# Output products of 14 of 18 token tiles by seven products of a Strassen level, with the output weights decoded earlier and kept in DRAM, and two first-layer units of 384 columns

## The chip, the cores and the metric

The kernel runs as one program on one core of a Trainium2 chip. The metric is the time of one execution on the device in microseconds (us): before the change three runs took 1123.82, 1124.44 and 1125.28 us, median 1124.44. Engines are named as in the profile: PE (matrix multiplication; PEld are its loads of the stationary operand), DVE (vector), ACT (scalar, activations), POOL (GpSimd) and SP (which issues the DMAs). SBUF is the on-chip memory, PSUM the eight banks into which PE accumulates, each 128 x 512 fp32.

## The reference

Attention with a bias made by a small network, then a layer `h - tanh(h)`, then a gated layer. Everything is fp32 at the interface; the weights come as float64.

```python
attn = softmax(q @ k.T / 8 + bias)            # 4 batches, 8 heads, 576 tokens, 64 wide
x = (attn @ v) as 2304 tokens x 512
h = x @ w_in;  x = (h - np.tanh(h)) @ w_out   # 512 -> 2048 -> 512
g = x @ w_gate                                # 512 -> 1536
silu = g * (1.0 / (1.0 + np.exp(-g)))
val = x @ w_val                               # 512 -> 1536
return silu * val @ w_out2                    # 1536 -> 512
```

## The kernel before, in words

Every product that needs fp32 accuracy is made of three PE instructions (`matmul3`, L719): both operands are split into a high part, rounded to PE's fp32r format, and the low rest; high x high, high x low and low x high are summed in PSUM. The split costs one cast on ACT (`scalar.copy`) and one subtraction on DVE or POOL (`subtract`, L64).

The first layer (class `Moe`, L746) takes the tokens in five units, `UNITS` (L734): four of 512 columns and one of 256. An item is one unit with one of the 16 chunks of 128 hidden columns. An item has 12 matmuls into `h` (`hidden`), a chain on ACT and DVE (`tanh_first`, `tanh_second`), the split of its result into `gh` and `gl` (`split`, L857 on ACT, L64 on POOL), and 12 matmuls into four banks `y` (`project`). Four chunks make a group; after each group the banks are added to `acc` in SBUF (L884). `ORDER` and `LAST_ORDER` (L735) are the order of the units in a group: the 256 unit third, in the last group first. `combine_x` (L984) queues the casts and subtractions that turn finished columns of `acc` into operands of the second layer; `flush(n)` emits n of them after each item (L1486).

The second layer (class `Second`, L945) works in 36 steps n: a set of 256 columns of the gate or value weights (set n // 3) against 768 tokens (n % 3). Steps 0 to 5 are plain blocks; from step 6 on (`step`, L1281) each 2 x 2 block product is done with seven products instead of eight, Strassen's scheme in Winograd's form. PE's order in a step is P1(n), P2(n-1), P4(n-1), P6(n), P3(n-1), P5(n), P7(n), with sums of partial results on ACT and DVE (`copy_one`, `copy_two`, `add`, `point_one`). `copy_two` (L1190) reads the bank into which P7(n) then accumulates. The gated result `s` goes to DRAM. The weights of a set are decoded from float64 bits to fp32 by two ACT, three DVE and one POOL instructions per 128 x 512 piece (`decode_first` L1052, `decode_second` L1063), then split and combined (`combine_w`). `plan_decode` (L1118) writes down for each set in which step and which part of the step (0, 1, 2) these stand.

The last product, `s` times `w_out2`, begins in `finish` (L1388). It has 18 token tiles of 128 and 12 chunks of 128 rows of `w_out2`; tiles are taken in waves of 8, 8 and 2, a stage is one chunk with one wave. `stage_load` brings `s` back from DRAM, `stage_split` casts and subtracts, and `out_tiles` multiplies: three matmuls of 512 columns for each tile and chunk. `w_out2` is decoded here too, one piece per step or stage from step 32 on (`FIRST_O`), and stays split in SBUF slots (`OUT_SLOTS`, `split_out`). `evict` copies a finished tile to SBUF and stores it. Each engine runs its instructions in the order in which this code emits them; the SP queue issues all DMAs in order.

Of the kernel before, what the change touches and what calls it, by code (L numbers as in the profile page):

```python
# [9 lines left out]
F32 = mybir.dt.float32  # L10
# [723 lines left out]
UNITS = [(0, 512), (512, 512), (1024, 512), (1536, 512), (2048, 256)]  # L734
ORDER, LAST_ORDER = (0, 1, 4, 2, 3), (4, 0, 1, 2, 3)  # L735
# [10 lines left out]
class Moe:  # L746
# [169 lines left out]
U2 = 384  # L916
# [5 lines left out]
OUT_SLOTS = (  # L922
    (16, 17), (18, 19), (27, 28), (29, 9), (20, 21), (22, 23), (24, 25), (26, 8), (0, 1), (2, 3), (4, 5), (6, 7),
)
QUAD_BANKS = (("h2", "h0", "h1"), ("h3", "y0", "y1"))
# [3 lines left out]
WAVES = ((0, 8), (8, 8), (16, 2))  # L929
LAST_C = 4  # L930
FIRST_O = 31
# [13 lines left out]
class Second:  # L945


    def __init__(self, tc, moe, weights, w_gate, w_val, w_out2, out):
# [7 lines left out]
        self.todo = [p for s in self.sets for p in s] + self.outs  # L956
# [7 lines left out]
    def pools(self, ctx):  # L964
        dram = ctx.enter_context(self.tc.tile_pool(name="c_dram", bufs=1, space=DRAM))
        self.s = [dram.tile([128, NT], F32, name=f"s_{c}") for c in range(FF2 // 128)]

# [16 lines left out]
    def combine_x(self, p):  # L984
# [28 lines left out]
        mixed = V if p == 2 else G  # L1013
# [97 lines left out]
    def split_out(self, c):  # L1111

        q = self.outs[c]
        q["pair"] = to = [self.columns(2 * at, 512) for at in OUT_SLOTS[c]]
        self.nc.scalar.copy(to[0], q["w"])
        subtract(self.nc, to[1], q["w"], to[0].bitcast(F32))

    def plan_decode(self):  # L1118
# [3 lines left out]
        for s in range(len(self.sets)):  # L1122
# [7 lines left out]
        for c, q in enumerate(self.outs):  # L1130
            n = FIRST_O + c
            add(n + 2, 0, self.split_out, c)
            add(n + 1, 1, self.decode_second, q)
            add(n + 1, 0, self.decode_first, q)
# [146 lines left out]
    def step(self, n):  # L1281
# [22 lines left out]
        if n == NQ - 1:  # L1304
            self.stage_split(0, 0, 768)
# [14 lines left out]
    def place(self, f, low):  # L1320

        return self.moe.x[low][:, f % 2, 0:1024]

    def raw(self, f):
        z = f % 3
        return self.moe.x[z // 2][:, 2 + z % 2, 0:1024].bitcast(F32)

    def stage_load(self, f, a=0, b=1024):

        if f >= len(self.stages):  # L1330
            return
        w, cs = self.stages[f]
        t0 = 128 * WAVES[w][0]
        if len(cs) == 1:
            self.nc.sync.dma_start(out=self.raw(f)[:, a:b], in_=self.s[cs[0]][:, t0 + a:t0 + b])
        else:
            n = 1024 // len(cs)
            for k, c in enumerate(cs):
                self.nc.sync.dma_start(out=self.raw(f)[:, n * k:n * k + n], in_=self.s[c][:, t0:t0 + n])

    def stage_split(self, f, a=0, b=1024):

        if f < len(self.stages):
            raw, hi, lo = self.raw(f)[:, a:b], self.place(f, 0)[:, a:b], self.place(f, 1)[:, a:b]
            self.nc.scalar.copy(hi, raw)
            subtract(self.nc, lo, raw, hi.bitcast(F32), self.nc.vector)

    def rows(self, at):

        z, k = divmod(at % 9, 3)  # L1350
# [4 lines left out]
    def out_tiles(self, f, ts=None):  # L1355

        nc = self.nc
        w, cs = self.stages[f]
        first, nt = WAVES[w]
        n = 1024 // len(cs)  # L1360
        s = self.place(f, 0), self.place(f, 1)
        for t in range(nt) if ts is None else ts:
            at = first + t
            if cs[0] == 0:
                self.o[at] = self.bank(OUT_BANKS[at % 8], f"o_{at}")
            for k, c in enumerate(cs):
                x = n * k + 128 * t
                matmul3(
                    nc, self.o[at], [a[:, x:x + 128] for a in s], self.outs[c]["pair"], c == 0, c == len(self.outs) - 1,
                )  # L1370
            if cs[-1] == len(self.outs) - 1:
                self.evict(at)
# [170 lines left out]
```

## Time and profile before

| | before |
|---|---|
| median of three runs | 1124.44 us |
| the profiled execution | 1124.47 us |
| its span, first to last instruction | 1122.7 us |
| PE busy | 1105.2 us, 98% of the span |
| DVE, ACT, POOL busy | 77%, 68%, 42% |
| mean granted clock | 0.999 |

The span is 1.8 us shorter than the execution. Busy time of PE is counted from the start of a matmul to its modelled end; matmuls overlap, so the pace of PE is read from start to start. First-layer items run from about 293 to 693 us, the steps of the second layer from 693 to 976 us, the output product from 968 us to the end.

### The profile page before, as it was taken

Reading aid. Unit: us, or ns where it says so; the run is one execution under the profiler, and the core shown is the slowest. Engines: PE = TensorE matmul, PEld = TensorE weight load, DVE = VectorE, ACT = ScalarE, POOL = GpSimd, SP = SyncE. Lnnn points to the kernel's source line nnn. Section 1 sums busy time; section 2 is a strip of 40 time slices with the busy share of each in tenths; the row PEclk is TensorE's granted clock in tenths of the full one; section 3 lists DMA queues with packets and bytes.
Section 4 is the critical chain, followed back from the end, with each engine's and each line's share of the span. In section 5 each row is a group of like instructions: output and inputs, shape, how many; then the busy total and the mean of one; then the engine's idle time right before and its main releaser. Section 6 shows DMA issues by size and latency. Waiting matters only on the chain.

```text
span 1122.7 us, 21424 instructions
## 1 busy us (share of the span) xinstructions
PE 1105.2 (98%) x7772; PEld 924.8 (82%) x7772; DVE 863.5 (77%) x1691; ACT 765.2 (68%) x1530; POOL 476.6 (42%) x499
## 2 busy tenths in 40 slices
PE   7999999999999999999999999999999999999998
PEld 3477777777688888888888888999999999988887
DVE  8978999999798889889988888987667665774222
ACT  7989999999698877777777776545455445453112
POOL 2367777777455355354434343124223222351000
PEclk9999999999999999999999999999999999999999
DMA  5863535351111111101101010131422422763433
GB/s 196 292 176 94 158 81 168 83 172 54 49 58 57 39 57 54 41 20 57 57 19 39 19 38 1 36 126 57 141 94 67 141 85 87 251 197 107 155 94 113
DMA packets 93034, 107.47 MB, mean 96 GB/s; under 512 B 45312, under 2 KB 72064, under 8 KB 92928
## 3 DMA queue, kind: packets, MB, share of 16 engines
q1 hardware_dynamic: 92928, 106.10, 30.1%
q8 instruction: 61, 1.00, 0.4%
q14 instruction: 45, 0.37, 0.1%
HBM read 75.41 MB, written 30.67 MB: 94 GB/s over the span
## 4 chain that ended last, share of the span: by engine, by line
PE 85%; DVE 8%; ACT 3%; issue 1%; POOL 1%; DMA 1%; DVEq 0%; ACTq 0%; POOLq 0%
PE b L722 19%; PE h L722 17%; PE y L722 16%; PE o L722 13%; PE x L438 7%; PE s L317 6%; PE pTa L383 2%; DVE acc L64 1%; PE pTb L383 1%; ACT p L343 1%; DVE r L146 1%; PE pE L400 1%; DVE p L332 1%; DVE xl L64 1%; DMA bias<-bev 1%
## 5 line engine op out<-in xcount | busy, mean ns | idle before, releaser
L722 PE MATMUL y<-gh,w 128*128 128x512 f32 (+1 forms) x748 | 197.0, 368 | 0.0
L722 PE MATMUL h<-xh,w 128*128 128x512 f32 (+1 forms) x640 | 191.0, 369 | 0.0
L722 PEld LDWEIGHTS y<-gh,w 128*128 128x128 f32 x748 | 133.9, 188 | 24.3 <-POOL gh L64 0.5
L722 PEld LDWEIGHTS h<-xh,w 128*128 128x128 f32 x640 | 116.9, 188 | 20.7 <-issue 0.4
L361 POOL TENSOR_SCALAR p<-p,r 128x576 f32<-128x576 f32 x144 | 109.7, 773 | 49.9 <-PE s L317 15.7
L722 PE MATMUL h<-xl,w 128*128 128x512 f32 (+1 forms) x320 | 117.9, 368 | 0.0
L343 ACT ACTIVATE p<-p,m 128x576 f32<-128x576 f32 x144 | 111.2, 775 | 1.2 <-DVE m L332 0.8
L332 DVE CUSTOM_DVE_ANT_0 p<-s,bt 128x576 f32<-128x576 f32 x144 | 103.7, 753 | 10.2 <-PE s L317 10.2
L722 PE MATMUL o<-w,xh 128*128 128x512 f32 x324 | 102.8, 389 | 0.0
L722 PE MATMUL b<-xh,w 128*128 128x384 f32 x360 | 101.4, 335 | 0.6 <-DVE sq L1211 0.6
L317 PEld LDWEIGHTS s<-k,q 64*128 64x128 f32 x768 | 57.7, 184 | 28.4 <-issue 17.6
L722 PE MATMUL y<-gl,w 128*128 128x512 f32 (+1 forms) x212 | 78.8, 372 | 0.9 <-POOL gl L64 0.9
L438 PE MATMUL x<-pt,vn 128*64 128x256 f32 (+1 forms) x512 | 79.0, 421 | 0.2 <-DVE xl L453 0.2
L317 PE MATMUL s<-k,q 64*128 64x288 f32 x768 | 73.1, 310 | 0.1
L64 POOL TENSOR_TENSOR gl<-g,gh 128x512 fp32r<-128x512 f32 (+1 forms) x27 | 33.3, 1232 | 90.2 <-issue 46.2
L722 PEld LDWEIGHTS o<-w,xh 128*128 128x128 f32 x324 | 60.8, 188 | 12.6
L722 PEld LDWEIGHTS h<-xl,w 128*128 128x128 f32 x320 | 60.3, 189 | 9.9
L722 PEld LDWEIGHTS b<-xh,w 128*128 128x128 f32 x360 | 65.9, 188 | 1.0 <-ACT acc21r L1104 0.9
L722 PE MATMUL b<-xl,w 128*128 128x384 f32 x180 | 60.1, 334 | 0.0
L831 ACT ACTIVATE sq<-h 128x512 f32<-128x512 f32 (+1 forms) x40 | 22.2, 556 | 50.6 <-PE h L722 50.6
L722 PE MATMUL o<-w,xl 128*128 128x512 f32 x144 | 56.2, 390 | 0.1
L168 PE MATMUL bps<-r,cst 128*32 128x512 f32 x264 | 48.3, 622 | 7.5 <-DVE r L146 5.3
(263 smaller groups left out, 2974.0 us busy)
## 6 DMA issues: line engine op xcount, KB each, us to landing
raw_out<-in_moe_w_out_dram SPq DMA_DIRECT2D x28, 512.0 KB, 3.5
bias<-bev SPq DMA_DIRECT2D x36, 320.0 KB, 3.3
bt<-bias SPq DMA_DIRECT2D x16, 576.0 KB, 4.9
s<-sq SPq DMA_DIRECT2D x24, 384.0 KB, 3.1
raw_in<-in_moe_w_in_dram SPq DMA_DIRECT2D x16, 512.0 KB, 3.7
xh<-s SPq DMA_DIRECT2D x15, 512.0 KB, 3.6
raw_gate<-in_moe_w_gate_dram SPq DMA_DIRECT2D x12, 512.0 KB, 3.6
raw_val<-in_moe_w_val_dram SPq DMA_DIRECT2D x12, 512.0 KB, 3.6
```

Source lines behind the costliest of these rows:

```text
L64: (engine or nc.gpsimd).tensor_tensor(out, a, b, ALU.subtract)
L146: nc.vector.tensor_scalar(r, src, b1, 0.0, ALU.add, ALU.max)
L168: nc.tensor.matmul(ps[0][32 * j:32 * j + 32].rearrange("p (t n) -> p n t", t=4), self.w2, R[j][:, 0:512].rearrange("p (n t) -> p n t", t=4 ...
L317: nc.tensor.matmul(self.st[u][j][:, e, 0:HALF], lhs, k[r, y, e * HALF:(e + 1) * HALF], start=n == 0, stop=n == 2,)
L332: nc.vector.tensor_tensor_reduce(out=p[:, n, :].rearrange("p (e f) -> p e f", e=2), in0=ps[n][:, :, 0:HALF], in1=bt[:, n, :].rearrange("p ...
L343: nc.scalar.activation(p[:, n, :], p[:, n, :], AF.Exp, bias=m[:, n:n + 1], scale=-1.0, accum_out=ls[:, n:n + 1],)
L361: nc.gpsimd.tensor_scalar(p[:, n, :], p[:, n, :], r[:, n:n + 1], 1.0, ALU.mult, ALU.mult)
L383: nc.tensor.transpose(half[h][:, 64 * m:64 * m + 64], p[r, j, k:k + 128], self.ident[r, r])
L400: self.nc.tensor.transpose(self.pt_end[:, at:at + 128], both, self.ident)
L438: nc.tensor.matmul(ps[r, 0:n], lhs, rhs, start=c == 0, stop=c == 4)
L722: nc.tensor.matmul(out, lhs[a], rhs[b], start=first and n == 0, stop=last and n == 2, skip_group_check=again)
L831: nc.scalar.activation(u, h, AF.Square)
```

## The change

`w_out2` is decoded earlier: `plan_decode` puts one piece into the steps of each set from set 5 on, and the last five into steps 31 to 34. `decode_out` stores a decoded piece to DRAM. The gate and value decode from set 5 on moves by up to a step, and a fourth place in a step, part 3, is used. In the output stage the waves are 4, 4, 4, 4 and 2 tiles. The first wave multiplies as before. The other 14 tiles are taken in pairs of tile halves with pairs of chunks (`out_products`): seven products of 256 columns in place of eight, with sums of `s` (S1 to S4) and of weights (T1 to T4). The weights come back from DRAM (`w_load`) and are split and summed by `w_split` in the first wave; `stage_split` forms the sums of `s` in every later stage; `gather` combines the seven products on DVE. `prepare` deals this work out between the matmuls.

In the first layer the last two units are 384 and 384 in place of 512 and 256, in plain order in every group; `flush(3)` becomes `flush(1)`, and in `combine_x` the four low parts that POOL subtracted go to DVE.

```diff
-UNITS = [(0, 512), (512, 512), (1024, 512), (1536, 512), (2048, 256)]
-ORDER, LAST_ORDER = (0, 1, 4, 2, 3), (4, 0, 1, 2, 3)
+UNITS = [(0, 512), (512, 512), (1024, 512), (1536, 384), (1920, 384)]
+ORDER, LAST_ORDER = (0, 1, 2, 3, 4), (0, 1, 2, 3, 4)
...
+OUT_FROM = 5
+OUT_LAST = (((31, 0), (31, 3)), ((31, 3), (32, 0)), ((32, 1), (33, 0)), ((33, 0), (33, 1)), ((34, 0), (34, 1)))
...
-WAVES = ((0, 8), (8, 8), (16, 2))
+WAVES = ((0, 4), (4, 4), (8, 4), (12, 4), (16, 2))
+OUT_PRODUCTS = (
+    ("P1", "A11", "B11"), ("P2", "A12", "B21"), ("P6", "S2", "T2"), ("P7", "S3", "T3"),
+    ("P5", "S1", "T1"), ("P3", "S4", "B22"), ("P4", "A22", "T4"),
+)
...
-        mixed = V if p == 2 else G
+        mixed = V
...
+    def decode_out(self, c):
+        q = self.outs[c]
+        self.decode_second(q)
+        self.nc.sync.dma_start(out=self.decoded[c], in_=q["w"])
...
+    def w_split(self, m, t):
...
+        sums = [lambda a=a: subtract(nc, *a, nc.vector) for a in (
+            (B11, B12, B11), (B12, B22, B12), (B22, B22, B11), (B21, B21, B22),
+        )]
...
+        hi = [lambda j=j: nc.scalar.copy(to[2 * j], raw[j]) for j in range(2)]
+        lo = [lambda j=j: subtract(nc, to[2 * j + 1], raw[j], to[2 * j].bitcast(F32), nc.vector) for j in range(2)]
+        return sums + hi + lo if t else hi + lo
...
-            when = ((n - 6, 1), (n - 5, 0), (n - 5, 1), (n - 4, 0), (n - 3, 0), (n - 3, 1), (n - 3, 1), (n - 2, 0))
+            when = ((n - 5, 0), (n - 5, 1), (n - 4, 1), (n - 4, 3), (n - 3, 0), (n - 3, 1), (n - 3, 1), (n - 2, 0))
...
+            if s >= OUT_FROM:
+                add(n - 5, 3, self.decode_first, self.outs[s - OUT_FROM])
+                add(n - 4, 0, self.decode_out, s - OUT_FROM)
...
+        high = [lambda j=j: nc.scalar.copy(cut(hi, j), src[j]) for j in range(4)]
+        low = [lambda j=j: subtract(nc, cut(lo, j), src[j], cut([a.bitcast(F32) for a in hi], j), nc.vector) for j in range(4)]
...
+        return [
+            high[1], high[0], sub(e[0], A11, A21), lambda: nc.vector.tensor_tensor(e[1], A21, A22, ALU.add), high[2], low[1],
+            sub(e[2], e[1], A11), low[0], sub(e[3], A12, e[2]), high[3], low[2], low[3],
+        ]
...
+        for k, a, b in OUT_PRODUCTS:
...
+            for q in range(pairs):
+                for i, m in enumerate(ms):
+                    x = 128 * (q if len(ms) == 1 else i)
+                    matmul3(
+                        nc, self.o[k][:, 256 * q:256 * q + 256], [c[:, x:x + 128] for c in names[a]], self.w[m][b],
+                        m == q == 0, m == len(W_PLACES) - 1, True,
+                    )
+            if ms[-1] == len(W_PLACES) - 1:
+                self.gather(w, k)
+            self.prepare(len(self.prep) // 6 + 1)
...
+            a, b, c = self.w_split(f + 2, 0), self.stage_split(f + 2), self.w_split(f + 1, 1)
...
+            self.prep += [lambda: self.w_load(f + 4), lambda: self.stage_load(f + 4)]
...
-            second.flush(3)
+            second.flush(1)
```

Where it moves instructions, first on ACT at the end of the first layer, before the change. `sq_78`, `s1_78` and so on belong to item 78, `gh_77` is the high part of item 77, `acc10` and `acc11` are sums of finished columns:

```order
971 L843 ACTIVATE kept_5955<-kept_5955,nc2_67 128x512
972 L1008 CAST xh_58<-acc10_5934 128x2x384
973 L1008 CAST xh_58<-acc11_5935 128x2x384
974 L831 ACTIVATE sq_78_9773<-h_78_9760 128x512
975 L832 ACTIVATE th_78_9774<-h_78_9760 128x512
976 L833 ACTIVATE s1_78_9775<-sq_78_9773,kq0_65 128x512
977 L834 ACTIVATE s2_78_9776<-sq_78_9773,kq1_66 128x512
978 L857 CAST gh_77_9781<-g_77_9733 128x512
```

and after it:

```order
971 L843 ACTIVATE kept_5967<-kept_5967,nc2_67 128x384
972 L1018 CAST xh_58<-acc10_5934 128x2x384
973 L831 ACTIVATE sq_78_9783<-h_78_9770 128x384
974 L832 ACTIVATE th_78_9784<-h_78_9770 128x384
975 L833 ACTIVATE s1_78_9785<-sq_78_9783,kq0_65 128x384
976 L834 ACTIVATE s2_78_9786<-sq_78_9783,kq1_66 128x384
977 L857 CAST gh_77_9791<-g_77_9745 128x384
```

One of the two casts ahead of item 78 is left, and since the units stand in another order the columns that it casts were finished a unit earlier.

Second on ACT in step 15, before the change (`b1_15` is the bank that `copy_two` reads into `u2_15`, `r_val6` a decode instruction of a later set):

```order
1100 L1092 CAST w5_5928<-bits_gate7_10859 128x512
1101 L1100 CAST acc21r_10250<-m_gate7_10914 128x256
1102 L1057 ACTIVATE r_val6_11000<-raw_val6_10846 128x512
1103 L1190 COPY u2_15_11011<-b1_15_10969 128x384
1104 L1195 COPY p5_15_11027<-b2_15_11020 128x384
```

and after it:

```order
1104 L1102 CAST w5_5928<-bits_gate7_10955 128x512
1105 L1110 CAST acc21r_10262<-m_gate7_10969 128x256
1106 L1263 COPY u2_15_11041<-b1_15_11005 128x384
1107 L1268 COPY p5_15_11057<-b2_15_11050 128x384
```

The decode instruction ahead of `copy_two` has gone to another step.

Third on DVE in the output stage: a stage of the first wave before (`bits_out` is a piece of `w_out2`, `xl` the low part of `s`):

```order
1601 L1059 TENSOR_SCALAR bits_out_12540<-raw_out_12394 128x512
1602 L1060 SCALAR_TENSOR_TENSOR bits_out_12540<-raw_out_12394,bits_out_12540 128x512
1603 L1068 SCALAR_TENSOR_TENSOR bits_out_12540<-m_out_12546,bits_out_12540 128x512
1604 L64 TENSOR_TENSOR xl<-xh 128x1024
```

and a stage of the first wave now (`wraw` are decoded weights from DRAM, `w`, `acc01r` their low parts; the numbers behind names are those of buffers):

```order
1640 L64 TENSOR_TENSOR wraw_2r<-wraw_2r 128x256
1641 L64 TENSOR_TENSOR w_5928<-wraw_12610,w_5928 128x512
1642 L64 TENSOR_TENSOR wraw_2r<-wraw_2m,wraw_2r 128x256
1643 L64 TENSOR_TENSOR w_5928<-wraw_12610,w_5928 128x512
1644 L64 TENSOR_TENSOR wraw_2m<-wraw_2m,wraw_2r 128x256
1645 L64 TENSOR_TENSOR xl<-xl,xh 128x512
1646 L64 TENSOR_TENSOR wraw_2m<-wraw_2m 128x256
1647 L64 TENSOR_TENSOR xl<-xh 128x512
1648 L64 TENSOR_TENSOR acc01r<-wraw_2r,acc01r 128x512
1649 L64 TENSOR_TENSOR w_5928<-wraw_2m,acc01r 128x512
```

DVE has ten instructions in such a stage, six of 512 and four of 256 elements, where it had four.

## Rows read from the trace of the kernel before

**Rows 1.** Part 1 of the page: busy us (share) x instructions.

```profile
PE 1105.2 (98%) x7772; PEld 924.8 (82%) x7772; DVE 863.5 (77%) x1691; ACT 765.2 (68%) x1530; POOL 476.6 (42%) x499
```

**Rows 2.** Stretches: busy us of PE, PEld, DVE, ACT, POOL; PEclk; DMA share; GB/s.

```profile
720.00:748.00 28.00, 27.38 (x157) 26.77 (x156) 25.36 (x35) 10.57 (x17) 6.41 (x7) 1.00 0.17 54
...
800.00:850.00 50.00, 50.00 (x289) 49.78 (x288) 35.16 (x58) 25.40 (x50) 14.62 (x15) 1.00 0.33 109
...
1000.00:1050.00 50.00, 50.00 (x222) 41.39 (x222) 23.01 (x24) 17.68 (x24) 10.11 (x7) 1.00 0.49 155
1050.00:1100.00 50.00, 50.00 (x222) 41.40 (x221) 12.04 (x12) 10.56 (x11) 0.00 (x0) 1.00 0.33 99
```

**Rows 3.** Waits of PE loads after 310 us: total, times, longest.

```profile
PEld b L722 <- ACT u L1190: 3.3, 6, 1.4
PEld y L722 <- POOL gl L64: 2.1, 4, 1.2
```

**Rows 4.** Timeline of PE, output stage: start, us, line, shape, count.

```profile
1085.28 0.39 PE L722 MATMUL o<-w,xl 128*128 128x512 f32 x1
...
1085.96 0.39 PE L722 MATMUL o<-w,xl 128*128 128x512 f32 x1
```

**Rows 5.** Timeline of PE, two items of the 256 unit.

```profile
601.12 0.28 PE L722 MATMUL h<-xh,w 128*128 128x256 f32 x1
...
603.99 0.28 PE L722 MATMUL y<-gh,w 128*128 128x256 f32 x1
```

**Rows 6.** Timeline of PE, a step of the second layer.

```profile
950.84 0.33 PE L722 MATMUL b<-xl,acc21r 128*128 128x384 f32 x1
...
951.36 0.33 PE L722 MATMUL b<-xl,acc21r 128*128 128x384 f32 x1
```

**Rows 7.** Loads of the stationary operand, by shape: busy, mean ns.

```profile
L722 PEld LDWEIGHTS h<-xh,w 128*128 128x128 f32 x640 | 116.9, 188 | 20.7 <-issue 0.4
```

**Rows 8.** Timeline, end of the first layer: ACT, PE, POOL.

```profile
684.27 0.84 ACT L1008 CAST xh<-acc 128x768 fp32r<-128x768 f32 x1 [2.45 <-DVE acc L884]
...
688.84 0.73 PE L722 MATMUL y<-gh,w 128*128 128x512 f32 x2
...
689.14 1.28 POOL L64 TENSOR_TENSOR gl<-g,gh 128x512 fp32r<-128x512 f32 x1 [6.51 <-ACT gh L857]
...
690.48 0.50 PE L722 MATMUL y<-gl,w 128*128 128x512 f32 x1 [0.91 <-POOL gl L64]
```

**Rows 9.** Timeline, step 9: ACT and PE loads.

```profile
776.20 0.67 ACT L1057 ACTIVATE r_val<-raw_val 128x512 int32<-128x512 uint32 x1
...
776.77 0.47 ACT L1190 COPY u<-b 128x384 f32<-128x384 f32 x1
...
777.29 1.01 PEld L722 LDWEIGHTS b<-w,acc20r 128*128 128x128 f32 x6 [0.23 <-ACT u L1190]
```

**Rows 10.** Timeline, DVE back to back: start, us for all.

```profile
661.20 2.74 DVE L884 TENSOR_TENSOR acc<-y,acc 128x256 f32<-128x256 f32 x8
...
682.95 2.48 DVE L884 TENSOR_TENSOR acc<-y,acc 128x512 f32<-128x512 f32 x4
```

**Rows 11.** DVE and POOL by shape after 700 us: busy, mean ns.

```profile
L64 DVE TENSOR_TENSOR xl<-xh 128x256 fp32r<-128x256 f32 x1 | 0.4, 426 | 0.9 <-ACT xh L1345 0.9
...
L1068 DVE SCALAR_TENSOR_TENSOR bits_out<-m_out,bits_out 128x512 f32<-128x512 f32 x12 | 8.3, 693 | 13.6 <-POOL bits_out L1061 13.4
...
L1061 POOL TENSOR_TENSOR bits_out<-bits_out,r_out 128x512 int32<-128x512 int32 x12 | 15.5, 1292 | 21.6 <-DVE bits_out L1060 19.6 <-PE b L722 2.0
```

**Rows 12.** DMA issues: count, KB each, median us to landing.

```profile
xh<-s SPq DMA_DIRECT2D x15, 512.0 KB, 3.6
```

**Rows 13.** Timeline of the end: PE, DVE, ACT.

```profile
1118.60 0.39 PE L722 MATMUL o<-w,xl 128*128 128x512 f32 x1
...
1119.02 0.42 DVE L1385 COPY rows<-o 128x256 f32<-128x256 f32 x1 [8.79 <-PE o L722]
...
1119.52 0.37 ACT L1385 COPY rows<-o 128x256 f32<-128x256 f32 x1 [2.63 <-DVE rows L1385]
```

More of the change, by code (lines that the diff above doesn't have):

```diff
@@ L966, in pools @@
         self.s = [dram.tile([128, NT], F32, name=f"s_{c}") for c in range(FF2 // 128)]
+        self.decoded = [dram.tile([128, 512], F32, name=f"s_w{c}") for c in range(FF2 // 128)]
     def columns(self, at, n):
@@ L1330, in stage_load @@
+    def stage_load(self, f):
         if f >= len(self.stages):
             return
[L1332 to L1346, printed above, removed]
+        w, ms = self.stages[f]
+        first, nt = WAVES[w]
+        half = 64 * nt
+        for j in range(2):
+            for k, m in enumerate(ms):
+                self.nc.sync.dma_start(
+                    out=self.raw(f, j)[:, :, half * k:half * k + half],
+                    in_=self.s[2 * m + j][:, 128 * first:128 * first + 2 * half].rearrange("p (h t) -> p h t", h=2),
+                )
@@ L1357, in out_tiles, with out_products @@
+    def out_products(self, f):
         nc = self.nc
-        w, cs = self.stages[f]
+        w, ms = self.stages[f]
         first, nt = WAVES[w]
[L1360 to L1372, printed above, removed]
@@ new lines, in gather, with store @@
+    def gather(self, w, k):
+        nc = self.nc
+        first, nt = WAVES[w]
+        pairs = nt // 2
+        n = 256 * pairs
+        two = lambda a: a.rearrange("p (q t) -> p q t", q=pairs)
+        ps = self.o.pop(k)[:, 0:n]
+        A, U2_, U3, U4 = (self.rows(at)[:, 0:n] for at in (2, 5, 6, 7))
+        R = [self.row_pair(z)[:, 0:pairs] for z in range(2)]
+        L, H_ = slice(0, 256), slice(256, 512)
+        plus = lambda to, a: nc.vector.tensor_tensor(to, ps if len(to.shape) == 2 else two(ps), a if len(to.shape) == 2 else two(a), ALU.add)
+        out = lambda z: self.out[128 * (first + pairs * z):128 * (first + pairs * z + pairs), :].rearrange("(q p) d -> p q d", p=128)
+        def store(z, *cols):
+            for c in cols:
+                nc.sync.dma_start(out=out(z)[:, :, c], in_=R[z][:, :, c])
+        if k == "P1":
+            nc.scalar.copy(A, ps)
+        elif k == "P2":
+            plus(R[0][:, :, L], A)
+        elif k == "P6":
+            plus(U2_, A)
+        elif k == "P7":
+            plus(U3, U2_)
+        elif k == "P5":
+            plus(R[1][:, :, H_], U3)
+            plus(U4, U2_)
+        elif k == "P3":
+            plus(R[0][:, :, H_], U4)
+            store(0, slice(0, 512))
+            if w == len(WAVES) - 1:
+                store(1, H_)
+        else:
+            plus(R[1][:, :, L], U3)
+            store(1, L if w == len(WAVES) - 1 else slice(0, 512))
```

183 lines of the change are left out of this document (132 added, 51 removed), and 3 rows, old and new, of the table W_PLACES.

## Prediction

> **What bounds the kernel now.** I read four views in this order: the busy times, the stretches, the list of waits, and the timeline where a term rests on it. The busy times show PE at 1105.2 us of a span of 1122.7 us, with DVE second at 77% [rows 1]. The stretches show the same stage by stage: in the steps of the second layer (800 to 850 us) and in the output stage (1000 to 1100 us) PE is busy without a gap, at the full granted clock [rows 2]. So from about 770 us on the time is the number of matmuls times their pace, and everything on DVE, ACT and POOL is hidden. The waits of PE loads after 310 us are few: 3.3 us in 6 waits for ACT's copy in `copy_two`, 2.1 us in 4 for POOL's `gl` [rows 3]. The reader is to see that only two things can move the time: fewer or shorter matmuls, and waits of PE that go or come.
>
> The pace is read from start to start. Three matmuls of 512 columns take 1085.96 - 1085.28 = 0.68 us, 0.2267 us each [rows 4]. Two items of the 256 unit are 24 matmuls, from 601.12 to 603.99: 2.87 / 24 = 0.1196 us each [rows 5]. Three of 384 columns take 951.36 - 950.84 = 0.52 us, 0.1733 us each [rows 6]. Half the columns thus cost 53% of the time, not 50%.
>
> **The output product: -8.8 us.** Before there are 18 tiles x 12 chunks x 3 = 648 matmuls of 512 columns: 648 x 0.2267 = 146.9 us. After, 4 tiles stay: 4 x 12 x 3 = 144, 32.6 us. The other 14 tiles are 7 pairs x 6 pairs of chunks x 7 products x 3 = 882 matmuls of 256 columns: 882 x 0.1196 = 105.5 us. Together 138.1 us, 8.8 us less. All of it is on the path, since PE has no gap there.
>
> The 378 additional loads of the stationary operand are counted in that pace. A load takes 188 ns in the rows [rows 7], longer than the 0.1196 us from one 256 matmul to the next [rows 5], so it is hidden behind matmuls already. The Trainium skill says otherwise for this form (TensorE: Matmul & The Clock Gate, The mechanism): loads overlap with running matmuls only where the row groups differ, and here all use all 128 rows. By that rule the loads would stand in line, and the fourth rival below gives its time. The trace speaks against it: 24 such matmuls, each with a new stationary operand, keep 0.1196 us.
>
> **The first layer: -1.7 us.** The matmuls cost nothing new: a unit of 512 and one of 256 have 0.2267 + 0.1196 = 0.3463 us for each pair of matmuls, two of 384 have 0.3467. What goes is waits. At its end ACT has two casts of finished sums ahead of item 78; the first begins at 684.27 after ACT stood idle for 2.45 us waiting for DVE's additions, and so POOL's `gl` comes late: PE starts matmuls at 688.84 and 0.23 us later, and the next only at 690.48, 690.48 - 689.07 - 0.23 = 1.2 us lost [rows 8]. In the new order that cast is of columns finished a unit earlier, one cast is emitted instead of two, and the last items are 384 wide. I take the whole 1.2 us as gone. The other three waits for `gl` make 2.1 - 1.2 = 0.9 us [rows 3]; the short 256 items, on which PE comes round soonest, are gone. I take 0.5 us of it. Against this DVE gets four subtractions that POOL did. They lie beside matmuls, and if they did not they would cost 4 x about 0.9 us; with both ends this term is -2.1 to +1.5 us.
>
> **The steps of the second layer: +0.2 us.** The decode instruction `r_val` ends just before `copy_two` on ACT at 776.77, and PE's load for P7 waits 0.23 us for that copy [rows 9]. The other three of this size come once in six steps. In the new order that instruction stands in another step, so I take 0.7 us of 4 x 0.23 = 0.9 us as gone. What comes is twelve pieces of `w_out2` in steps 10 to 34: three DVE, two ACT and one POOL instruction each, at most 0.69 us on DVE [rows 11], 12 x 3 x 0.69 = 24.8 us on DVE. Steps of the second layer have 50.00 - 35.16 = 14.8 us of idle DVE in 50 us [rows 2], about 54 us in 25 steps of 7.3 us (42 matmuls x 0.1733). So they fit; but at part 3 of one step in three DVE's last decode instruction now stands right behind POOL's addition of the same piece, which takes 1.29 us [rows 11], and `add` is queued behind it on DVE, `sigmoid_pair` and the next `copy_one` behind that on ACT. P6 of the next step, which needs `copy_one`, begins 42 + 18 matmuls, 10.4 us, after such a step does; that queue ends, by my estimate from the durations in [rows 9, 11], about 1 us ahead of it. Lower end 0, upper end all seven such waits, 7 x 1.29 = 9.0 us; I take 0.9 us, near the lower end, because the idle share is wide.
>
> **Handover and first wave: +1.7 us.** This is the term I know least. In a stage of the first wave PE has 4 tiles x 2 chunks x 3 = 24 matmuls, 5.44 us. DVE has six instructions of 512 and four of 256. Back to back it does eight of 256 in 2.74 us and four of 512 in 2.48 us [rows 10]; less the last one's own 0.43 and 0.69 us [rows 11] that is a pace of (2.74 - 0.43) / 7 = 0.33 us and (2.48 - 0.69) / 3 = 0.60 us. By pace a stage is 6 x 0.60 + 4 x 0.33 = 4.9 us, and the first wave (four such stages, one of 5 x 0.60 + 9 x 0.33, one of 5 x 0.60 + 5 x 0.33 with two copies of results) 30.3 us against PE's 32.6: hidden. By full durations it is 36.4 us: 3.8 us not hidden. Which end holds depends on how often DVE waits for ACT's casts, for DRAM (3.6 us to landing [rows 12]) and for the step before. DVE prepares two stages ahead, so up to a stage of lag is free. Ends 0 and 3.8; I take 1.7. In the later waves DVE has 5 x 0.33 + 3 x 0.60 = 3.5 us of sums and low parts in a stage of 42 x 0.1196 = 5.0 us, and in each wave's last stage seven additions from PSUM more, 4.2 us, a lag of 2.7 us that the two stages of lead hold. Their DMAs move 512 KB a stage, as before, so I cost them at nothing; if this cover goes, a late load costs PE about what its landing takes, 3.6 us.
>
> **The end: -0.4 us.** The last matmul starts at 1118.60, DVE copies one half (1119.02, 0.42 us), ACT the other from 1119.52 [rows 13], then both go out. After, one DVE addition of 256 and one store: ACT's 0.37 us go.
>
> **Sum.** -8.8 - 1.7 + 0.2 + 1.7 - 0.4 = -9.0 us. The profiled execution took 1124.47 us (span 1122.7 us and 1.8 us around it), 0.03 us off the median of the three runs. 1124.5 - 9.0 = 1115.5 us.
>
> **The rivals.**
> First, DVE bounds the first wave. For it: ten DVE instructions a stage that each wait for a cast or a load. Against it: the pace in [rows 10] and the lead of two stages. Price: the whole 3.8 us beside the 1.7 us of the handover, which then come from the steps before: 1119.3 us, still faster.
> Second, waits at the start of the second layer go too. Steps 4 to 7 wait because decode, casts and sums crowd DVE (25.36 of 28.00 us, 720 to 748 us [rows 2]) and ACT; 3.3 - 0.9 = 2.4 us of the waits for `copy_two` [rows 3] are there, and with starts of refilled matmuls 3.1 us. POOL's four subtractions are gone from there and half of the casts come earlier. Against it: sets 2 to 4 are decoded in the same steps as before. 1115.5 - 3.1 = 1112.4 us.
> Third, and slower: the decode amid gate and value. DVE, in order, stands behind POOL's addition (1.29 us) and the three instructions of the extra piece (up to 2.1 us), 3.4 us in each of seven groups of three steps. If half of it reaches PE, 7 x 1.7 = 11.9 us in place of the 0.9 taken: 1126.5 us. It is slower than before from (9.0 + 0.9) / 7 = 1.4 us a group on. For it: PE already waited for `copy_two` in this stage. Against it: 6.5 us of idle DVE in three steps by [rows 2].
> Fourth, slower: the loads bound the 256 matmuls at their 188 ns [rows 7]: 882 x (0.188 - 0.1196) = +60.3 us, 1175.8 us. Against it stand [rows 5].
>
> **Chances.** Forecast 0.60, its own range 1113.5 to 1118; first rival 0.22; second 0.09; third 0.06; fourth 0.01; a mixture that ends where it began 0.02. A measurement of this kernel can tell about 0.2% (2.2 us) from no change. Faster by more: 0.60 + 0.22 + 0.09 = 0.91; within: 0.02; slower: 0.06 + 0.01 = 0.07. The range that holds 8 in 10 goes from the second rival's 1112.4, rounded down to 1112, past the first rival's 1119.3 with 2.2 us of the steps' upper part: 1121.5 us.
>
> **What would show it.** The `o` matmuls of 256 columns should start 0.12 us apart and number 882, the stage from the last step to the end should be about 9 us shorter less its waits. The wait for `gl` at the end of the first layer and the waits for `copy_two` in steps 9, 15, 21 and 27 should be gone, and the first layer should end 1 to 2 us earlier. If PE's loads wait for DVE's `xl` or `w` in the first wave, the first rival holds; if for `copy_one`, `copy_two` or `add` in steps 10 to 34, the third. I am wrong if the 256 matmuls do not keep 0.12 us, or if PE shows more than 4 us of new waits.

## The result, and the profile after

The changed kernel takes 1115.06 us (median of 4 runs, 1114.23 to 1116.90), the kernel before 1124.63 us (4 runs, 1123.82 to 1125.28). The ratio is 0.9916, with a 95% interval of 0.9903 to 0.9928. The forecast was 1115.5 us. The profiled execution took 1115.4 us, its span is 1113.6 us.

Part 1 of the page after, answering to [rows 1]; PE is busy 8.0 us less, and DVE, at 77% before, is at 84%:

```profile
PE 1097.2 (99%) x8150; PEld 952.8 (86%) x8150; DVE 935.7 (84%) x1916; ACT 790.6 (71%) x1606; POOL 452.4 (41%) x483
```

Where the time went is read best by adding up, for each stage, the time from each matmul's start to the next one's:

| stage | before, us | after, us | measured | forecast |
|---|---|---|---|---|
| up to the first matmul of the first layer | 292.65 | 292.18 | -0.47 | 0 |
| first layer (h, y) | 398.01 | 396.61 | -1.40 | -1.7 |
| matmuls of the attention between the first items | 7.97 | 7.96 | -0.01 | 0 |
| plain steps of the second layer (c) | 51.08 | 51.38 | +0.30 | |
| steps by products (b) | 221.76 | 221.50 | -0.26 | +0.2 with the line above |
| output product (o) | 147.13 | 139.84 | -7.29 | -8.8 + 1.7 = -7.1 |
| start of the last matmul to the end | 4.06 | 4.10 | +0.04 | -0.4 |
| span | 1122.66 | 1113.57 | -9.09 | -9.0 |

The first line is no work of the change: up to there PE, DVE, ACT and POOL have the same instructions in all kernels shown here, and yet the first matmul of the first layer started anywhere from 291.66 to 294.44 us in their profiled executions. Small effects are therefore read from the stages below, not from the times. Where an edit leaves a stage alone, its trace agrees with the changed kernel's within 0.1 us in h and y, in c and in b, and within 0.3 us in o.

The stretches after, by the columns of [rows 2]:

```profile
core 0: us, PE busy (x) PEld busy (x) DVE busy (x) ACT busy (x) POOL busy (x), PEclk, DMA share, GB/s
720.00:748.00 28.00, 26.99 (x154) 26.38 (x153) 25.36 (x37) 11.77 (x19) 6.21 (x6) 1.00 0.22 72
800.00:850.00 50.00, 50.00 (x290) 49.81 (x289) 37.20 (x64) 28.05 (x56) 17.03 (x18) 1.00 0.42 141
975.00:1008.00 33.00, 31.85 (x159) 26.93 (x157) 31.48 (x66) 19.31 (x36) 0.00 (x0) 1.00 0.56 184
1000.00:1050.00 50.00, 48.85 (x398) 48.22 (x397) 44.40 (x96) 23.46 (x46) 0.00 (x0) 1.00 0.46 148
1050.00:1100.00 50.00, 50.00 (x419) 50.00 (x419) 43.64 (x93) 21.72 (x42) 0.00 (x0) 1.00 0.38 122
```

PE is full from 800 us on but for one gap of over 0.2 us. In the part of the first wave from 975 to 1008 us DVE is busy for 31.48 of 33 us, so it has next to nothing to spare. The waits of PE's loads after 310 us (us in total, times, longest), answering to [rows 3]:

```profile
PEld b L722 <- ACT u L1263: 2.9, 5, 1.4
PEld oP L722 <- DVE rows L1479: 1.4, 1, 1.4
PEld b L722 <- ACT acc21r L1114: 0.9, 1, 0.9
PEld c L722 <- DVE kept L1284: 0.8, 1, 0.8
PEld y L722 <- POOL gl L64: 0.5, 2, 0.3
PEld y L722 <- POOL gh L64: 0.5, 1, 0.5
PEld b L722 <- DVE sq L1284: 0.2, 1, 0.2
```

The waits for `gl` fell from 2.1 to 0.5 us, the one of 1.2 us at the end of the first layer [rows 8] is gone. The wait for DVE's `rows` is new. The 256 matmuls in the middle of the output stage, with their loads:

```profile
1060.15 0.28 PE L722 MATMUL oP<-w_two,xl 128*128 128x256 f32 x1
1060.27 0.40 PE L722 MATMUL oP<-w_two,xh 128*128 128x256 f32 x2
1060.51 0.28 PE L722 MATMUL oP<-w_two,xl 128*128 128x256 f32 x1
...
1060.03 0.19 PEld L722 LDWEIGHTS oP<-w_two,xl 128*128 128x128 f32 x1
```

Three matmuls from 1060.15 to 1060.51: 0.12 us each, as in [rows 5], with loads of 0.19 us. The trace has 882 of them.

### The profile page after: what moved, and what is told of

Its sections match the earlier page's. It is cut to its first block, busy times and chain, and to the rows that moved or that the text cites. A ratio compares the mean times of both kernels' runs of the same rounds, so it can differ in the third digit from the quotient of the medians.

```text
span 1113.6 us, 22605 instructions
## 1 busy us (share of the span) xinstructions
PE 1097.2 (99%) x8150; PEld 952.8 (86%) x8150; DVE 935.7 (84%) x1916; ACT 790.6 (71%) x1606; POOL 452.4 (41%) x483
## 4 chain that ended last, share of the span: by engine, by line
PE 82%; DVE 10%; ACT 2%; issue 1%; POOL 1%; DMA 0%; SPq 0%; DVEq 0%; ACTq 0%; POOLq 0%
PE b L722 19%; PE h L722 17%; PE y L722 17%; PE oP L722 9%; PE x L438 7%; PE s L317 6%; PE pTa L383 2%; DVE r L146 1%; DVE xl L64 1%; DVE acc L64 1%; PE pTb L383 1%; ACT p L343 1%; DVE w L64 1%; PE pE L400 1%; PE bps L168 1%
## 5 line engine op out<-in xcount | busy, mean ns | idle before, releaser
L722 PE MATMUL h<-xh,w 128*128 128x512 f32 (+1 forms) x640 | 193.8, 368 | 0.0
L722 PEld LDWEIGHTS y<-gh,w 128*128 128x128 f32 x748 | 137.6, 188 | 18.0 <-POOL gh L64 0.5
L1436 ACT CAST xh<-ext 128x512 fp32r<-128x512 f32 x42 | 26.1, 621 | 44.1 <-DVE ext L64 24.7
L419 DVE COPY pt<-pTb 128x512 f32<-128x512 f32 (+1 forms) x80 | 50.7, 633 | 5.3 <-PE pTb L383 3.9
L722 PE MATMUL oP<-w,xh 128*128 128x256 f32 x280 | 55.0, 283 | 0.0
```

Of the source, the lines that this page charges most:

```text
L419: copy(to, src)
L722: nc.tensor.matmul(out, lhs[a], rhs[b], start=first and n == 0, stop=last and n == 2, skip_group_check=again)
L1436: high = [lambda j=j: nc.scalar.copy(cut(hi, j), src[j]) for j in range(4)]
```

## The experiments

Each kernel is the changed one with the edit shown; all were timed against the kernel before.

**The output product alone.** `a2_plain` multiplies every wave as the first one.

```diff
-        if not self.stages[f][0]:
+        if True:
...
-            if f < ms:
-                self.out_plain(f, range(4) if f else range(2, 4))
-            else:
-                self.out_products(f)
+            self.out_plain(f, range(WAVES[self.stages[f][0]][1]) if f else range(2, 4))
```

> The changed kernel with all 18 token tiles multiplied plainly in 512 columns; the weights still come decoded from DRAM, and the sums and low parts of the weights that Strassen's products need are still formed, though nothing reads them. By the forecast's theory the output matmuls alone carry the gain: 648 x 0.2267 = 146.9 us in place of the 139.8 us that the stage took after, less the DVE wait of 1.4 us at the border of the first two waves that may stay or go: +7 to +8.8 us, 1122.1 to 1123.9 us, and the stage shows 147 us. Rival: a part of the gain comes from where the decode stands and from the weights kept in DRAM: then under +5 us, below 1120 us. By the rival that the 256 matmuls lose to their loads, this kernel would be no slower than the changed one.

Measured: 1122.93 us (11 runs), ratio to before 0.9983 (0.9974 to 0.9992); the output stage takes 146.74 us, and there is no wait at the border of the waves. The products are worth 146.74 - 139.84 = 6.9 us in the trace, where the wait that the changed kernel has at that border is already taken off, and 7.9 us in the medians. The rest of the change brings 1.8 us in the medians; in the output stage it is 147.13 - 146.74 = 0.4 us.

**What ended the waits of the first layer.** Three runs put back one part each: the units with their orders, the number of queued casts and subtractions handed out per item, and POOL's subtractions.

```diff
-UNITS = [(0, 512), (512, 512), (1024, 512), (1536, 384), (1920, 384)]
-ORDER, LAST_ORDER = (0, 1, 2, 3, 4), (0, 1, 2, 3, 4)
+UNITS = [(0, 512), (512, 512), (1024, 512), (1536, 512), (2048, 256)]
+ORDER, LAST_ORDER = (0, 1, 4, 2, 3), (4, 0, 1, 2, 3)
```

> The changed kernel with the first layer's units of 512, 512, 512, 512 and 256 columns and their two orders put back. The changed kernel took 1115.1 us. By the forecast's theory the units and their order are worth the waits for gl alone: the 1.2 us wait in the last items of the first layer comes back and some of the other three, in all +1.4 us (what the trace shows from the first h matmul to the end of the y matmuls: 398.0 us before, 396.6 us after), 1116.5 us, and the wait stands at about 690 us again. Rival A: the wait went because fewer casts are handed out at the end of an item (one and not three) and because DVE took over the subtractions of POOL, not because of the units: then +0.0 to +0.3 us, 1115.2 us, and no wait of over 0.5 us at the end of the first layer. Rival B: the old order moves work into the second layer's first steps too: over +2.5 us.

```diff
-            second.flush(1)
+            second.flush(3)
```

> The changed kernel with three queued casts or subtractions handed out at the end of each first-layer item, as before, in place of one. With the old units the wait at the end of the first layer did not come back (the h and y matmuls took 396.64 us, the changed kernel 396.61 us, the kernel before 398.01 us), so the units are not what removed it. Theory: it was the burst on ACT, two casts ahead of the last items' work; then with three at a time a wait of about 1.2 us for POOL's gl stands at 680 to 692 us again and the h and y matmuls take about 397.9 us, +1.2 us. Rival A: it was POOL's subtractions (the other run of this pair): then no wait here, 396.6 us. Rival B: the burst matters only with the last items 512 wide, so neither run of the pair brings it back.

```diff
-        mixed = V
+        mixed = V if p == 2 else G
```

> The changed kernel with the four low subtractions of B21 and B22 for the first two thirds of the tokens put back on POOL from DVE. Theory: POOL does them in its queue ahead of gl and gh of the last items, and each takes longer than on DVE, so gl comes late: the wait of about 1.2 us for gl at 680 to 692 us is back, the h and y matmuls take about 397.9 us in place of 396.6 us, and DVE, freed of them, lets the waits at 732 and 746 us (1.34 us in all in the changed kernel) shrink: in sum -0.5 to +1.2 us. Rival (the forecast's reason): ACT's burst of casts made gl late: then no wait for gl here beyond the 0.2 us at 655 us.

Measured: 1117.17 us (units), 1117.96 us (hand-out) and 1116.00 us (POOL), 5 runs each, ratios 0.9938, 0.9936 and 0.9918. POOL's subtractions are worth nothing in the first layer (h and y take 396.56 us) and 0.2 us in the plain steps (c takes 51.57 us). Units and hand-out together make this table (h and y + c, in us; the kernel before also has POOL's subtractions and the old places of the decode, so its cell differs by more than units and hand-out):

| | 3 per item | 1 per item |
|---|---|---|
| units of 512 and 256 | 398.01 + 51.08 = 449.09 (before) | 396.64 + 52.33 = 448.97 |
| units of 384 and 384 | 399.87 + 50.12 = 449.99 | 396.61 + 51.38 = 447.99 (changed) |

Handing out one at a time removes the waits of the first layer with either units. With the old units the cast ahead of the last items starts without a wait, since DVE's additions, which it waited for before [rows 8], now come behind it; ACT and DVE in that run:

```profile
682.13 0.83 ACT L1018 CAST xh<-acc 128x768 fp32r<-128x768 f32 x1
...
683.37 2.49 DVE L884 TENSOR_TENSOR acc<-y,acc 128x512 f32<-128x512 f32 x4
```

So it is a cast of columns finished earlier, as the forecast had it, but because the queue is worked off more slowly. Of the 24 casts from `acc`, 8 are done before the plain steps in the kernel before, 4 in this run, 6 in the changed kernel and 8 with three at a time. What is not cast in the first layer is cast in the plain steps, where PE then waits for DVE; with the old units that gives nearly all of 1.4 us back, with the new ones 1.3 of 3.3 us. The waits of PE, two rows of POOL and two of DVE in the run with three at a time:

```profile
PEld y L722 <- POOL gl L64: 2.9, 4, 1.5
PEld y L722 <- POOL gh L64: 1.3, 1, 1.3
...
664.10 1.30 POOL L1071 TENSOR_TENSOR bits_val<-bits_val,r_val 128x512 int32<-128x512 int32 x1 [3.71 <-DVE bits_val L1070]
665.34 1.28 POOL L64 TENSOR_TENSOR gl<-g,gh 128x512 fp32r<-128x512 f32 x1
...
656.16 0.94 DVE L64 TENSOR_TENSOR xl<-acc,xh 128x768 fp32r<-128x768 f32 x1
661.07 1.82 DVE L64 TENSOR_TENSOR xl<-acc,xh 128x768 fp32r<-128x768 f32 x2
```

The same `gl` starts at 663.28 us in the changed kernel. It is late because the decode instruction ahead of it on POOL starts only at 664.10 us, after 3.71 us of idle for DVE; in the changed kernel that one starts at 662.02 us. DVE has three subtractions of the queue ahead of its part of that decode (from 656.16 and 661.07 us), where the changed kernel has one (at 659.88 us). So by the trace it is the burst on DVE that costs here, and not the casts on ACT that the expectation named; no run parts the two.

**The wait at the first border of waves.**

```diff
-                (self.nc.vector.tensor_copy if t in (1, 2) else self.nc.scalar.copy)(row, self.o[t])
+                self.nc.scalar.copy(row, self.o[t])
```

> The changed kernel with ACT, not DVE, copying the results of tiles 1 and 2 of the first wave out of PSUM. In the changed kernel PE waits 1.31 us (and loses 0.10 us at the start) at 1007.97 us for the bank that DVE empties at 1007.23 us, late. Theory: DVE is late because the preparation for two stages ahead stands before the copy in its queue, and ACT, at 19.3 us of 33 us busy in that wave, is not: the wait goes, -1.4 us, 1113.7 us, and the o matmuls take 138.4 us in place of 139.8 us. Rival A: the wait moves to the next thing that DVE brings late (low parts of the first products, the additions from PSUM): 0 to -0.5 us, with a wait for DVE of about 1 us in the following 10 us. Rival B: ACT's casts come late behind its copies: a wait of the same size for ACT's xh or w, 0 or worse.

Measured: 1114.92 us (4 runs, ratio 0.9914), which the time alone can't tell from 1115.06; the output stage takes 138.71 us in place of 139.84. The lost 1.31 us shrank to 0.18 us, now for ACT. The cause is seen on DVE in the changed kernel, with the matmul that waits:

```profile
1005.02 0.68 DVE L1479 COPY rows<-o 128x512 f32<-128x512 f32 x1
1005.63 0.68 DVE L64 TENSOR_TENSOR xl<-xh 128x512 fp32r<-128x512 f32 x1
1006.23 0.42 DVE L64 TENSOR_TENSOR ext<-ext,xl 128x256 f32<-128x256 f32 x1
1006.56 0.42 DVE L64 TENSOR_TENSOR xl<-xl,xh 128x256 fp32r<-128x256 f32 x1
1006.90 0.42 DVE L64 TENSOR_TENSOR ext<-xh,ext 128x256 f32<-128x256 f32 x1
1007.23 0.68 DVE L1479 COPY rows<-o 128x512 f32<-128x512 f32 x1
...
1007.97 0.39 PE L722 MATMUL oP<-acc21r,xh 128*128 128x256 f32 x1 [1.15 <-DVE rows L1479]
```

DVE has no idle; four instructions for stages ahead stand between the two copies, and P4 needs the bank that the second one empties. Whether it would be enough to put the copies ahead of these four was not tried.

**How full DVE is in the first wave.**

```diff
-                self.prep = [*a[:2], *b[:2], c[0], a[2], c[1], a[3], c[2], c[4], b[2], c[3], c[5], b[3], c[6], c[7]]
+                self.prep = [*a[:2], *b[:2], c[0], a[2], c[1], a[3], a[3], c[2], c[4], b[2], c[3], c[5], b[3], c[6], c[7]]
```

> The changed kernel with one subtraction of 512 columns on DVE done twice in each of the first four stages of the first output wave (the second writes the same values): 4 x 0.60 = 2.4 us more DVE work. In the changed kernel DVE runs without idle from about 988 to 1010 us, and PE waits 1.31 us for its last copy. Theory (the first rival of the forecast, that DVE bounds the first wave, holds to that extent): the added work passes to PE nearly whole, the wait grows to 3 to 3.7 us or is split, and the o matmuls take 141.9 to 142.3 us in place of 139.8 us, +2 to +2.4 us. Rival: DVE's idle in stages 1 and 2 (966 to 988 us: 19.3 of 21.5 us busy) and the lead of two stages take it: under +0.7 us.

Measured: 1119.14 us (5 runs, ratio 0.9942); the output stage takes 142.18 us, +2.34 us for 2.4 us of work. (The medians differ by 4.1 us; the profiled execution began the first layer 1.6 us later than the changed kernel's, which makes most of the rest. The two runs with one repeated addition, below, began it 1.65 and 1.4 us later.) The added time comes as new waits for low parts beside the old one:

```profile
PEld oP L722 <- DVE rows L1479: 1.9, 2, 1.4
PEld o L722 <- DVE xl L64: 1.8, 4, 0.7
```

**How near the steps were to the third rival.** The addition behind P3 is repeated in the seven steps with a decode instruction at part 3: four times, and once.

```diff
-            self.add(n - 1, 0, 2, "u2")
+            for _ in range(5 if n % 3 == 2 and 11 <= n <= 29 else 1):
+                self.add(n - 1, 0, 2, "u2")
```

> The changed kernel with DVE's addition behind P3 done five times in place of once, in the seven steps 11, 14, ... 29 in which the last decode instruction stands at part 3 (the repeats write the same values). It puts 4 x 0.47 = 1.9 us into DVE's queue ahead of the sigmoid and the next copy_one on ACT. In one such step of the changed kernel copy_one ends at 851.56 us and P6, which needs it, starts at 852.73 us, 1.17 us later. Theory of the forecast's third term: what is over this slack reaches PE: 7 x (1.9 - 1.2) = 4.9 us, and PE's loads wait for ACT's copy b or for DVE; 1120 us. Rival A: the idle share of DVE takes it all, 0 to +0.5 us. Rival B: the whole delay reaches PE, 7 x 1.9 = 13 us, because other waits of PE have no slack (the addition also empties a bank that P5 needs).

Measured: 1130.30 us (5 runs), slower than before by 0.4%, ratio 1.0038 (1.0024 to 1.0052); b takes 236.74 us, +15.2 us. Rival B was nearest. PE's waits:

```profile
PEld b L722 <- DVE sq L1274: 7.1, 3, 2.4
PEld b L722 <- DVE v L1274: 5.6, 4, 1.4
```

They are not for `copy_one`, as expected, but for DVE's next addition (`add`, L1274), which empties the bank of P4. In the changed kernel, at step 15:

```profile
813.30 0.69 DVE L1078 SCALAR_TENSOR_TENSOR bits_gate<-m_gate,bits_gate 128x512 f32<-128x512 f32 x1 [1.46 <-POOL bits_gate L1071]
813.90 0.55 DVE L1274 TENSOR_TENSOR sq<-b,u 128x384 f32<-128x384 f32 x1
814.37 0.55 DVE L1274 TENSOR_TENSOR sq<-b,p 128x384 f32<-128x384 f32 x1
...
815.15 1.03 PE L722 MATMUL b<-w 128*128 128x384 f32 x5
```

DVE stood 1.46 us behind POOL's addition, the addition for P4 ended at 814.37 + 0.55 = 814.92, and P4 started at 815.15: 0.23 us to spare. Before, the same difference was 1.27 us in step 15; after, it is 0.21 to 0.23 us in steps 15, 21 and 27 and 0.90 to 1.20 us in 12, 18, 24 and 30. P6, behind `copy_one`, has 0.47 to 0.49 us to spare in the first three and 1.42 us in the other four; the 1.17 us of the expectation were read in step 20, where the addition has not yet stood behind a decode at part 3.

> The changed kernel with DVE's addition behind P3 done twice in place of once in the seven steps 11, 14, ... 29 (the second writes the same values). With four repeats PE waited 1.23 us in each of four of the following steps and 2.2 us in three, for DVE's next addition, which empties the bank that P4 needs, and in two places the matmuls after it ran at half the granted clock. In the changed kernel the start of P4 less the end of that addition is 1.20, 0.90, 1.18 and 1.19 us in steps 12, 18, 24 and 30 and 0.23, 0.21 and 0.23 us in steps 15, 21 and 27, of which 0.05 us is there even where PE waits. Theory: one repeat is 0.59 us; it is hidden in the four steps and leaves 0.59 - 0.18 = 0.41 us and 0.11 us at the start in the three: +1.6 us in the matmuls of the second layer (221.5 us in the changed kernel, 223.1 us), no stretch at a lower clock. Rival A: the idle of DVE ahead of it (1.46 us, waiting for POOL) takes it: 0. Rival B: each of the seven steps pays about 0.6 us: +4 us.

Measured: 1118.60 us (5 runs, ratio 0.9934); b takes 223.20 us, +1.7 us: three waits of 0.42 to 0.45 us in steps 15, 21 and 27, none in the other four.

```profile
PEld b L722 <- DVE sq L1274: 1.8, 3, 0.6
```

```diff
-            when = ((n - 5, 0), (n - 5, 1), (n - 4, 1), (n - 4, 3), (n - 3, 0), (n - 3, 1), (n - 3, 1), (n - 2, 0))
+            when = ((n - 5, 0), (n - 5, 1), (n - 4, 1), (n - 3, 0), (n - 3, 0), (n - 3, 1), (n - 3, 1), (n - 2, 0))
```

> As the run with one repeated addition, and the last decode of a set's second piece stands at part 0 of the next step, no longer at part 3. Theory: the slack of P4 in steps 15, 21 and 27 (0.23 us) is small because DVE waits 1.46 us for POOL at part 3 ahead of the two additions; with that instruction behind them the slack is above 1 us again, the repeat is hidden, and the matmuls of the second layer take 221.5 us or 0.2 us less (the three waits of 0.11 us may go). Rival A: the instruction, now ahead of point_one's work on DVE, makes the bank of P4 or the copy for P7 late: new waits of 0.3 us or more in steps 9 to 30, 222.5 us or more. Rival B: the slack has another cause and the 1.6 us of the other run stay.

Measured: 1119.23 us (5 runs, ratio 0.9943). The slack of P4 is 1.25 us or more in all seven steps, so the instruction at part 3 did take it, but rival A came: waits of 0.24 us for `copy_two` in the same seven steps, and b takes 223.86 us. The row beside the 2.9 us of the changed kernel:

```profile
PEld b L722 <- ACT u L1263: 5.4, 10, 1.4
```

**The waits at steps 6 and 7, and a version with the gains together.** Two decode entries of the fourth set are moved first; then this edit, that of the copies and earlier stores are put together.

```diff
-    4: ((6, 1), (7, 1), (8, 0), (8, 1), (9, 0), (9, 1), (9, 1), (10, 0)),
+    4: ((6, 3), (7, 3), (8, 0), (8, 1), (9, 0), (9, 1), (9, 1), (10, 0)),
```

> The changed kernel with two entries of the table of early decodes moved: the first and second decode of the fourth set's first piece from part 1 of steps 6 and 7 to part 3, behind copy_two of the same step. In the changed kernel PE waits 0.87 us at 752.33 us and 1.21 us at 760.92 us (and 0.11 us each at the start) for ACT's copy u, which stands behind decode instructions on ACT that wait for POOL. Theory: with the decode behind the copy both waits go, -2.3 us at most, and -1.5 us with what comes new, 1113.6 us. Rival A: in step 7 set 3's sums also stand ahead of the copy, so only the first wait goes: -1.0 us. Rival B: the later decode makes set 4 late, or makes the copies of P5 and the sigmoid of that step late: a new wait of 1 us or more for ACT or DVE in steps 6 to 12, 0 or slower.

Measured: 1115.04 us (4 runs, ratio 0.9916). The waits at 752 and 761 us are gone, but 0.30 us for DVE at 762.29 us and 0.88 us for `copy_two` at 767.47 us came: b takes 220.69 us, 0.8 us less, which the medians (1115.04 and 1115.06) don't show. The decode ahead of the copy was the cause of the two waits. More than half of their cost came back as the new ones, of the kind that rival B had named, but smaller.

```diff
         elif k == "P2":
             plus(R[0][:, :, L], A)
+            if w == len(WAVES) - 1:
+                store(0, L)
...
             plus(U4, U2_)
+            if w == len(WAVES) - 1:
+                store(1, H_)
         elif k == "P3":
             plus(R[0][:, :, H_], U4)
-            store(0, slice(0, 512))
-            if w == len(WAVES) - 1:
-                store(1, H_)
+            store(0, H_ if w == len(WAVES) - 1 else slice(0, 512))
```

> The changed kernel with three edits: ACT copies the results of tiles 1 and 2 of the first wave; the two entries of the early decodes stand at part 3; and in the last wave the stores go out as soon as each quarter is ready (the left half of the upper rows after P2, the right half of the lower rows after P5), so that only two stores are left behind the last two products where three were. Theory: the first two add up as their traces showed, -1.1 and -0.8 us; in the last, SP issued three stores one after the other at 1109.66 and from 1110.06 us, about 0.4 us each, and the last left some 0.4 us late: -0.3 us. Sum -2.2 us, 1112.9 us. Rival A: the end of the span is set by the landing of the last store and not by its issue: nothing for the third, 1113.2 us. Rival B: the edits trade waits among themselves: above 1114.5 us.

Measured: 1113.96 us (4 runs, 1113.55 to 1115.35), ratio 0.9901 (0.9887 to 0.9914): 1.1 us under the changed kernel in the medians, with intervals that overlap. From the first matmul of the first layer to the end its trace takes 819.07 us, the changed kernel's 821.39: -2.32 us, of it -0.85 in b, -0.85 in o and -0.59 at the end. DVE's last addition and SP's last issues, changed kernel:

```profile
1109.66 0.34 SPq L1520 DMA_DIRECT2D out_dram<-kept  x1
1109.78 0.42 DVE L1515 TENSOR_TENSOR rows<-oP,rows 128x256 f32<-128x256 f32 x1 [0.15 <-PE oP L722]
1110.06 0.91 SPq L1520 DMA_DIRECT2D out_dram<-rows  x2
```

and combined kernel:

```profile
1110.20 0.33 SPq L1520 DMA_DIRECT2D out_dram<-kept  x1
1110.32 0.42 DVE L1515 TENSOR_TENSOR rows<-oP,rows 128x256 f32<-128x256 f32 x1 [0.15 <-PE oP L722]
1110.77 0.33 SPq L1520 DMA_DIRECT2D out_dram<-rows  x1
```

In the first the issues of the last two stores end at 1110.06 + 0.91 = 1110.97, 1.50 us after the last matmul's start (1109.47); in the second at 1111.10, 1.09 us after it (1110.01). That is 0.41 of the 0.59 us; the rest lies behind the issue.

With two handed out per item in the same kernel:

```diff
-            second.flush(1)
+            second.flush(2)
```

> The combined kernel (ACT copies the first wave's results, two decode entries behind copy_two, early stores in the last wave) with two queued casts or subtractions handed out per item at the end of the first layer, in place of one. One gave 396.6 us for the h and y matmuls and 51.4 us for the first steps (c), three gave 399.9 and 50.1 us. Theory: waits in the first layer grow with the burst on ACT and waits for DVE in the first steps shrink with what is done earlier; two lies between: h and y 397 to 398 us, c 50.1 to 50.5 us, in sum -0.3 to +0.6 us against the combined kernel. Rival: two is enough to empty the queue in time and short enough for ACT: -1.2 us. Other rival: the first burst alone costs, as with three: +1.5 us.

Measured: 1118.09 us (5 runs, ratio 0.9940). Worse than every expectation: h and y take 401.69 us, +5.1 us, and c 50.13 us, -1.3 us. Two per item is not between one and three. In its trace the subtractions come in pairs on DVE (at 655.85, 666.51 and 678.5 us), and PE loses 0.6 to 1.7 us at a time from 666.6 us on, in the items behind each pair. That the pairs cause it is likely, and was not separated further.

## Why the prediction was right, and where its terms were not

The total agrees with the span's difference to 0.1 us, and a part of that is luck. Of the -9.09 us, -0.47 lie ahead of the first layer, where the change does nothing; the stages behind it moved by -8.6 us. The first layer and the end fell short by 0.3 and 0.4 us, the steps and the output stage did better by 0.2 us each.

**The output product.** Right, and `a2_plain` shows that the products carry it. The 882 matmuls take 107.12 us, less 1.41 us at the border of the waves 0.1199 us each, where [rows 5] gave 0.1196: 0.2 us over all. By a line of the Trainium skill (TensorE: Matmul & The Clock Gate, The mechanism) loads overlap only where row groups differ; the trace does not agree, since loads of 0.19 us stand behind matmuls 0.12 us apart. The fourth rival is out. (Its price took the loads behind one another; loads that also stood in line with the matmuls would have cost more.)

**Handover and first wave.** Its size came out: 139.84 us stand against 138.1 us of matmuls, 1.7 us more as forecast, of it 1.41 us at the border of the waves and the rest pace. That is luck, as the 1.7 us were picked between ends of 0 and 3.8 us and not added up from anything. The forecast looked for waits for `xl` or `w`; it was the copy of a result behind that work. The mechanism is the first rival's, DVE at its bound: 2.4 us more of its work cost 2.34 us, and the 2.3 us to spare in the forecast's sum by pace (30.3 against 32.6 us) were not there. The rival's 3.8 us, a sum by full durations, did not come, since the pace of [rows 10] held (0.33 and 0.6 us between the starts in the rows around 1006 us). In the later waves PE has no wait, so their DMAs did cost nothing.

**The first layer.** The wait of 1.2 us went as forecast, and the stage gained 1.4 us of 1.7; the 0.5 us for the other three waits for `gl` hardly came, since beside the 1.3 us of the long wait and the refill behind it the stage gained 0.1 us. The reason was half right: one cast handed out instead of two removes the long wait, the units don't. What the step missed is the second half of the same edit: the work not done there is done in the plain steps, +0.3 us net. And the units, costed by their matmuls at nothing, are worth 1.0 us with one at a time, all of it in the plain steps: 6 casts are done before these in place of 4. With three at a time they were worth nothing (449.99 against 449.09 us, in kernels that differ by more than the units).

**The steps.** +0.2 forecast, +0.04 measured over c and b. Of the 0.7 us for `copy_two` only the wait of step 9 went (0.21 us by the starts); in steps 15, 21 and 27 the loss fell from about 0.19 to 0.14 us each. The 0.9 us of new waits did not come. The estimate of about 1 us to spare named the wrong consumer: behind a decode at part 3 it is 1.42 or 0.47 us for P6, but 0.9 to 1.2 or 0.23 us for P4. The third rival's mechanism is real: DVE does stand 1.46 us behind POOL, and what is over the slack reaches PE, in the run with four repeats with 15.2 us. The change stayed clear of it by 0.23 us in three steps.

**The end.** The forecast's -0.4 us did not come. ACT's copy is gone, but the last product's store is the third in a line on SP; the change issues three stores behind the last two products. Two, and the end is 0.59 us shorter. Every DMA that a moved step issues had to be counted here.

**The second rival.** Wrong: the waits at steps 6 and 7 (0.87 and 1.21 us) are as before, since sets 3 and 4 are decoded in the same places. Its reason turned out the other way round: fewer casts are done before the plain steps, 6 in place of 8.

## What to carry to other kernels

Where PE is full, a term of matmuls can be forecast closely from start-to-start rows of the same shape (here 138.1 us, and 138.4 us without the wait), while the waits around it depend on which consumer of a late engine comes first: take the slack at each of them (start of the consumer less end of the producer) before an edit is costed as hidden. An edit that spreads work out removes waits in one stage and may put them into the next, so it is read over both, and two edits of one queue are tested together as well as alone. At the end of a kernel, count the stores that queue behind the last result.

## What was not expected of the hardware

In the run with four repeats PE stood idle for 2.0 us in full flow until 820.13 and until 869.09 us, and behind each of these waits the granted clock fell, 1.4 and 0.2 us after PE was busy again. The stretches around the first, and some matmuls in it:

```profile
820.10:821.60 1.50, 1.47 (x8) 1.47 (x9) 1.08 (x2) 1.50 (x4) 0.00 (x0) 0.98 0.00 0
821.60:824.90 3.30, 3.30 (x13) 3.30 (x12) 2.20 (x4) 1.88 (x5) 2.29 (x3) 0.50 0.00 0
824.90:830.00 5.10, 5.10 (x31) 5.10 (x31) 2.66 (x5) 2.94 (x6) 0.10 (x1) 0.99 0.01 3
...
918.00:925.00 7.00, 6.97 (x39) 6.79 (x40) 5.01 (x8) 4.88 (x11) 2.42 (x3) 1.00 0.00 0
```

```profile
822.97 0.53 PE L722 MATMUL b<-xh,acc21r 128*128 128x384 f32 x1
823.29 0.53 PE L722 MATMUL b<-xl,acc21r 128*128 128x384 f32 x1
823.61 0.84 PE L722 MATMUL b<-xh,acc21r 128*128 128x384 f32 x2
```

From 821.6 to 824.9 us the granted clock is 0.50, the lower of its two levels (1.2 GHz), and matmuls of 384 columns start 0.32 us apart where at the upper level (2.4 GHz) it is 0.173 us [rows 6]; some ten of them lose 1.6 us, and 1.7 us behind the second wait. The third wait of 2.0 us, until 918.02 us, had no such stretch behind it, and none of the four waits of 1.2 us had. So a wait of 2 us can cost most of itself again, and doesn't always.
